# Two float16 sums moved from GpSimd to VectorE, loads one half further ahead and a store on ScalarE's queue, in a retention and PReLU kernel

## The chip, the core and the metric

One core of a Trainium2 chip runs the kernel. The metric is the device time of one execution in microseconds (us). The core's engines are named as in the profile: PE (TensorE matmuls) with PEld (its weight loads), DVE (VectorE), ACT (ScalarE), POOL (GpSimd) and SP (SyncE, which here only issues DMAs).

## What is computed

A retention recurrence over 768 tokens for 4 batches and 8 heads of width 64, then a two-layer network on all 3072 tokens:

```python
for t in range(S):
    state = gamma[None, :, None, None] * state + np.einsum('bhd,bhe->bhde', k[:, :, t], v[:, :, t])
    y[:, :, t] = scale * np.einsum('bhd,bhde->bhe', q[:, :, t], state)
x = np.ascontiguousarray(y.transpose(0, 2, 1, 3)).reshape(B * S, H * D)
h = x @ w_in                                              # 512 -> 2048
g = np.maximum(h, 0.0) + alpha * np.minimum(h, 0.0)
out = g @ w_out                                           # 2048 -> 512
```

## The kernel before

**Units, halves, blocks.** The 3072 tokens are 12 units of 256 (three to a batch). A unit has two halves, so there are 24 halves, numbered `w` from 0 to 23 in the code; from `w` = 8 on a half is 128 tokens of all heads. Two units make a block of 512 tokens; there are six blocks, `n` = 0 to 5. The recurrence is computed in chunks: products within a chunk, and a state carried from chunk to chunk.

**The way of a half.** `load` (L145) issues three DMAs on SP's queue, for k, q and v. `prep` (L190) scales k and q into float16 on POOL (four instructions at L201), issues a DMA transpose on SP's queue (L224) that waits for them, and casts v on POOL (L231). `both` (L570) then runs on PE the products of one unit that is finished ("old": L614, L590) and of one that begins ("new": scores L638, state sums L652). Its DVE part follows: the mask (L695) and six small instructions that make the next states (L707 to L713). The next call of `both` reads those states on PE at L590.

**The two layers.** `ffn1` (L739) makes, for each of 16 slices of 128 of the 2048 features, a product of four matmuls into one of eight PSUM banks (L780). ACT writes relu of its negative (L736, three buffers), and DVE joins both into `gt`, float16 (the PReLU, L725). In the prediction "PReLU 0" to "PReLU 15" are these DVE instructions of a block, in order. Blocks 0 and 1 take the second layer as plain matmuls (`ffn2`). Blocks 2 to 5 take it as seven products of half-size parts (`sevens`, L866), a Strassen scheme: `gt` falls into four quarters a11 (features 0 to 7, first 256 tokens), a21 (same features, other tokens), a12 and a22 (features 8 to 15), and these sums are needed:

- s3 = a11 - a21 (called `three[n]`, L1148), read by product 7;
- s2 = a22 - s3 (L918) and s1 = a21 + a22 (L919), for products 6 and 5;
- s4 = a12 - s2 (L927), for product 3.

Each sum is two instructions of 128x1024 float16 elements (`combine`, L845, recorded at L848). Before the change s2 and s1 run on DVE; s3 of blocks 2 to 5 and s4 of blocks 2, 3 and 4 run on POOL; s4 of block 5 runs on DVE.

**The order.** It is written out by hand: each engine executes its instructions in the order in which the program issues them, and generators (`tick`) interleave the two layers with the rest. In a block from 2 on, the first layer's 64 matmuls are issued in two lots of 20 with an `ahead` call after each; then the 40 that have been issued are ten slices, s3 follows, then the last 24. After it the products come in the order 1, 7, `both`, 2, 4, 5, the first four matmuls of 6, `both`, the rest of 6, and 3 (block 4 has the second `both` without a new unit; block 5 has the products 1, 7, 2, 6, 5, 4, 3 and no `both`). Product 1 writes the PSUM bank that slice 10 of the first layer used, and product 7 that of slice 14, so product 7 waits for PReLU 14.

`ahead(m)` (L1111) preps the next m halves and then issues the load of the half two further on for each. Block 2 preps halves 14 and 15 in its first layer, 16 and 17 beside the products; block 3 preps 18, 19 and then 20, 21; block 4 preps 22 and 23. SP takes its queue strictly in order, so a load that is issued behind a transpose waits until POOL has made what that transpose reads.

**The end.** In block 5 the results leave in stores of 256 x 256 (`store`, L911), the last of them, c12, cut in three, of which the second is issued by ACT and the others by SP.

Of the kernel before, what the change touches and what calls it, by code (L numbers as in the profile page):

```python
# [15 lines left out]
SUB = mybir.AluOpType.subtract  # L16
# [3 lines left out]
def kernel(  # L20
# [16 lines left out]
    nc = tc.nc  # L37
# [6 lines left out]
    NW = 2 * B * NUS  # L44
# [95 lines left out]
    def place(w):  # L140
        u, g = divmod(w, 2)
        b, c3 = divmod(u, NUS)
        return u, g, b, c3

    def load(w, which="kqv"):  # L145
        u, g, b, c3 = place(w)
        t = staged.setdefault(w, {})
        for nm in which:
            src = {"k": k, "q": q, "v": v}[nm]
            t[nm] = sbp.tile([128, 4, 2 * D], FP, tag=f"{nm}s", bufs=8, name=f"{nm}s{w}")  # L150
            if w < NPE:
                nc.sync.dma_start(
                    out=t[nm],
                    in_=src[b, 4 * g : 4 * g + 4, TU * c3 : TU * c3 + TU, :].rearrange(
                        "h (p a) d -> p h (a d)", a=2
                    ),
                )
            else:
                at = TU * c3 + 128 * g
                nc.sync.dma_start(  # L160
                    out=t[nm].rearrange("p a (b d) -> p (a b) d", b=2),
                    in_=src[b, :, at : at + 128, :].rearrange("h p d -> p h d"),
                )
# [675 lines left out]
    three = {}  # L839
# [5 lines left out]
    def combine(eng, out, one, two, op, at=(0, 4)):  # L845
        for i in at:
            cut = slice(i, i + 4)
            eng.tensor_tensor(out=out[:, cut], in0=one[:, cut], in1=two[:, cut], op=op)  # L848
# [17 lines left out]
    def sevens(n, ts, last=False):  # L866

        gt = gts.pop(n)  # L870
        a11, a21, a12, a22 = [quarter(gt, i, j) for i in range(2) for j in range(2)]
        ss = {1: a11, 2: a12, 4: a22, 7: three.pop(n), 5: new_part("s1"), 6: new_part("s2")}
        banks = {}
        cuts = [(0, 0, 256), (1, 0, 128), (1, 128, 128)]

        def product(m, at, start):
            steps = [(kt, t, 0, 256) for kt in range(8) for t in range(2)]
            split = last and m in (5, 3)
            if split:
                steps = [(kt, *cut) for cut in cuts for kt in range(8)]  # L880
            for i, (kt, t, c, w) in enumerate(steps):
                to = (t, c) if split else at
                first = start and i in ((0, 8, 16) if split else (0,))
                if first:
                    banks[to] = ps("ops", {(0, 0): at, (1, 0): "pb", (1, 128): "s"}[to] if split else at)
                z = 256 * t + c
                nc.tensor.matmul(  # L887
                    out=banks[to][:, z : z + w],
                    lhsT=ss[m][:, kt, 128 * t : 128 * t + 128],
                    rhs=ts[m][:, kt, c : c + w],  # L890
                    start=first,
                    stop=(kt == 7),
                    skip_group_check=True,
                )
                if i % 2:
                    yield

        def piece(name):
            return sbp.tile([128, 512], FP, tag="os", bufs=7, name=name)

        def copied(at, name):
            x = piece(name)
            nc.scalar.activation(out=x, in_=banks[at], func=COPY, bias=0.0, scale=1.0)  # L903
            return x

        def added(eng, name, one, two, cut=slice(0, 512), x=None):
            x = piece(name) if x is None else x
            eng.tensor_tensor(out=x[:, cut], in0=one[:, cut], in1=two[:, cut], op=ADD)  # L908
            return x

        def store(x, i, j, t=slice(0, 2), c=slice(0, 256), on=None):  # L911
            row = TB * n + 256 * i
            (on or nc.sync).dma_start(
                out=out[row : row + 256, 256 * j : 256 * j + 256].rearrange("(t p) c -> p t c", p=128)[:, t, c],
                in_=x.rearrange("p (t c) -> p t c", t=2)[:, t, c],
            )

        combine(nc.vector, ss[6], a22, ss[7], SUB)  # L918
        combine(nc.vector, ss[5], a21, a22, ADD)  # L919
        by = "f" + "ba"[flip["f"]]  # L920
        at = "fb" if by == "fa" else "fa"
        yield from product(1, at, True)
        x1 = copied(at, "x1")
        yield from product(7, by, True)
        x7 = copied(by, "x7")
        ss[3] = new_part("s4")
        combine(nc.vector if last else nc.gpsimd, ss[3], a12, ss[6], SUB)  # L927
        yield from product(2, at, False)
        store(copied(at, "c11"), 0, 0)
        if last:  # L930
            yield from product(6, "pa", True)
            u2 = added(nc.vector, "u2", banks["pa"], x1)
            yield from product(5, at, True)
            y = piece("y5")
            for t, c, w in cuts:
                z = 256 * t + c
                added(nc.vector, "", banks[t, c], x7, slice(z, z + w), y)
            store(added(nc.gpsimd, "c22", y, u2), 1, 1)
            yield from product(4, by, False)
            store(added(nc.vector, "c21", banks[by], u2), 1, 0)  # L940
            c12 = piece("c12")
            for i, _ in enumerate(product(3, at, False)):
                if i % 4 == 3:
                    t, c, w = cuts[i // 4]
                    z = 256 * t + c
                    added(nc.vector, "", banks[t, c], u2, slice(z, z + w), c12)
                    store(c12, 0, 1, slice(t, t + 1), slice(c, c + w), nc.scalar if i == 7 else None)
                yield
            return
        yield from product(4, by, False)  # L950
        x74 = copied(by, "x74")
        yield from product(5, at, True)
        y = added(nc.vector, "y5", banks[at], x7)
        yield from product(6, by, True)
        u2 = added(nc.vector, "u2", banks[by], x1)
        store(added(nc.gpsimd, "c21", x74, u2, x=x74), 1, 0)
        store(added(nc.gpsimd, "c22", y, u2, x=y), 1, 1)
        yield from product(3, at, False)
        store(added(nc.vector, "c12", banks[at], u2), 0, 1)
        flip["f"] = by != "fa"  # L960

    def tick(gen, m):
        for _ in range(m):
            if next(gen, 1) == 1:
                return
# [89 lines left out]
    gen = ffn1(0, "ffyppsYffSppyfsY", 2)  # L1055
# [36 lines left out]
    gen = ffn2(0, ((0, 1, 2), (3,)), ("fa", "fb", "pa", "fa"), held=held)  # L1092
# [18 lines left out]
    def ahead(m=1):  # L1111
        ws = [w for w in range(more[0], more[0] + m) if w < NW]
        for w in ws:
            prep(w)
        for w in ws:
            if w + 2 < NW:
                load(w + 2)
            while w >= 12 and held:
                to, src = held.pop(0)
                nc.sync.dma_start(out=to, in_=src)  # L1120
        more[0] += m
# [6 lines left out]
    gen = ffn1(1, "1y023Y1023sy1S0Y", 6)  # L1128
# [6 lines left out]
    for n in range(1, NBLK):  # L1135
        if n > 1:
            gen = ffn1(n, "fspyfSpY" if n == 2 else "syfSpYfp")
        for i in range(2):
            tick(gen, 10 if n == 1 else 20)
            ahead()  # L1140
            if n == 1 and i == 0:
                next(todo)
        if n == 2:
            ts = next(todo)
        if n > 1:
            three[n] = new_part("s3")
            low, late = [quarter(gts[n], 0, j) for j in range(2)]
            combine(nc.gpsimd, three[n], low, late, SUB)  # L1148
        for _ in gen:
            pass  # L1150
        if n == 1:
            gen = ffn2(n)
        else:
            gen = sevens(n, ts, n + 1 == NBLK)
        u0 = 2 * (n + 1)
        if n + 1 < NBLK:
            early = n == 1
            tick(gen, 2)
            if early:
                both(None, u0)  # L1160
            if early:
                next(todo)
            ahead(2)
            tick(gen, 24 if early else 14)
            both(u0, u0 + 1)
            if early:
                next(todo)
            tick(gen, 26)
            both(u0 + 1, u0 + 2 if 2 * u0 + 4 < NW else None)
        for _ in gen:  # L1170
            pass
# [30 lines left out]
```

## Time and profile before

| | |
|---|---|
| time, median of 3 runs | 200.85 us (200.27, 200.85, 200.94) |
| time of the profiled execution | 200.22 us |
| its span, first to last instruction | 198.5 us |
| PE busy | 191.3 us, 96% of the span |
| DVE busy | 150.1 us, 76% |
| POOL busy | 132.1 us, 67% |
| ACT busy | 97.2 us, 49% |
| granted PE clock | full in every one of 40 slices |
| POOL, one s3 instruction (L848) | 2129 ns (median of 8) |
| POOL, one s4 instruction (L848) | 2119 to 2567 ns, median 2175 (6 of them) |
| DVE, the same kind of sum (L848) | 679 to 3052 ns, median 684 |

How to read it: busy time is the time in which an engine had an instruction in flight. For PE that includes the tail of a pipelined matmul, so where PE lost time is read from stretches of equal work, not from its share. The difference between the execution's own time and its span, 1.7 us, lies before the first and after the last instruction of the program. The stages of the two layers, as used in the prediction, begin with the first L780 matmul of a block (first layer) and the first L887 matmul (products).

### The profile page before, as it was taken

What the parts mean: (1) busy time and instruction counts of PE and PEld (TensorE: products, weight loads), DVE (VectorE), ACT (ScalarE), POOL (GpSimd) and SP (SyncE); (2) the same over time, 40 slices, a digit from 0 to 9 for tenths busy, and PEclk for the clock granted to TensorE, in tenths of its full rate; (3) what the DMA queues carried; (4) which work ended last, traced back from release to release, by engine and by line L of the source; (5) the groups of instructions that cost most, each with busy time, mean ns of one, the idle gap of its engine ahead of it and who ended that gap; (6) DMA issues with size and microseconds to landing.
All of it is one profiled execution on the core that took longest, in us unless ns stands there. A gap on an engine that the chain in (4) does not pass through costs nothing. (4 is left out here: it accounts for less than half of the span.)

```text
span 198.5 us, 6106 instructions
## 1 busy us (share of the span) xinstructions
PE 191.3 (96%) x2535; PEld 122.1 (62%) x2535; DVE 150.1 (76%) x242; ACT 97.2 (49%) x166; POOL 132.1 (67%) x161
## 2 busy tenths in 40 slices
PE   6889999999999999999999999998999999999992
PEld 2667445556885455444788544887544888445892
DVE  3575887655789956788996788999988854788842
ACT  2585776245676232576353367252366352566300
POOL 3489796858799982399996699981499271371020
PEclk9999999999999999999999999999999999999999
DMA  5999999999999969999639969999263010400014
GB/s 157 319 341 338 392 376 387 395 319 222 212 226 203 230 117 217 301 315 221 153 72 222 243 189 172 224 116 237 77 196 73 0 56 3 160 0 3 0 56 159
DMA packets 90476, 38.21 MB, mean 192 GB/s; under 512 B 68288, under 2 KB 85840, under 8 KB 90448
## 3 DMA queue, kind: packets, MB, share of 16 engines
q1 hardware_dynamic: 90128, 37.69, 74.1%
q8 instruction: 20, 0.33, 0.7%
q10 hardware_dynamic: 320, 0.12, 0.3%
q14 instruction: 8, 0.07, 0.1%
HBM read 27.32 MB, written 6.29 MB: 169 GB/s over the span
## 5 line engine op out<-in xcount | busy, mean ns | idle before, releaser
L725 DVE SCALAR_TENSOR_TENSOR gt<-hm,oma,hps 128x512 f16<-128x512 f32 (+1 forms) x112 | 73.1, 670 | 13.6 <-ACT hm L736 4.8
L736 ACT ACTIVATE hm<-hps 128x512 f32<-128x512 f32 x96 | 57.2, 597 | 32.7 <-PE hps L780 28.6
L780 PE MATMUL hps<-xT,win 128*128 128x512 f16 x320 | 70.3, 379 | 0.1
L780 PEld LDWEIGHTS <-win 128*128 128x128 f16 x320 | 31.2, 98 | 37.3 <-issue 0.6
L805 PE MATMUL ops<-wout,gt 128*128 128x512 f16 x128 | 29.3, 379 | 0.0
L887 PEld LDWEIGHTS <-s 128*128 128x128 f16 x272 | 25.2, 98 | 2.8
L201 POOL TENSOR_TENSOR kdq<-ks,tab 128x256 f16<-128x256 f32 x32 | 19.9, 642 | 9.2 <-DMA ks<-in_k_dram 8.9
L887 PEld LDWEIGHTS <-gt 128*128 128x128 f16 x192 | 18.5, 98 | 3.2
L805 PEld LDWEIGHTS <-gt 128*128 128x128 f16 x128 | 11.9, 98 | 13.2
L848 POOL TENSOR_TENSOR s<-gt 128x1024 f16<-128x1024 f16 x8 | 16.9, 2129 | 4.7 <-DVE gt L725 4.7
L201 POOL TENSOR_TENSOR kdq<-qs,tab 128x256 f16<-128x256 f32 x32 | 19.4, 629 | 0.6 <-DMA qs<-in_q_dram 0.6
L848 POOL TENSOR_TENSOR s<-gt,s 128x1024 f16<-128x1024 f16 x6 | 13.5, 2266 | 4.6 <-PE ops L887 3.9
L887 PE MATMUL ops<-wout,s 128*128 128x256 f16 (+1 forms) x136 | 15.3, 266 | 0.0
L887 PE MATMUL ops<-wout,gt 128*128 128x256 f16 x128 | 15.3, 273 | 0.0
L887 PE MATMUL ops<-t,s 128*128 128x256 f16 (+1 forms) x136 | 15.3, 266 | 0.0
L763 PE MATMUL hps<-xT,win 128*128 128x256 f16 x128 | 15.2, 273 | 0.0
L908 POOL TENSOR_TENSOR x<-x,u 128x512 f32<-128x512 f32 x3 | 3.8, 1271 | 15.8 <-DVE u L908 12.5
L695 DVE TENSOR_TENSOR m<-sc,mi 128x1024 f16<-128x1024 f32 x8 | 9.8, 1219 | 4.7 <-PE sc L638 4.7
L763 PEld LDWEIGHTS <-win 128*128 128x128 f16 x128 | 12.0, 98 | 2.0
L824 ACT ACTIVATE os<-ops 128x512 f32<-128x512 f32 x8 | 4.7, 596 | 16.1 <-PE ops L805 14.8
L188 POOL CAST wout<-wo 128x512 f16<-128x512 f32 x16 | 10.3, 660 | 2.9 <-DMA wo<-in_moe_w_out_dram 2.8
L903 ACT ACTIVATE x<-ops 128x512 f32<-128x512 f32 x11 | 6.6, 596 | 9.4 <-PE ops L887 9.4
(90 smaller groups left out, 229.5 us busy)
## 6 DMA issues: line engine op xcount, KB each, us to landing
ks<-in_k_dram SPq DMA_DIRECT2D x24, 256.0 KB, 4.6
qs<-in_q_dram SPq DMA_DIRECT2D x24, 256.0 KB, 4.8
vs<-in_v_dram SPq DMA_DIRECT2D x24, 256.0 KB, 4.5
wi<-in_moe_w_in_dram SPq DMA_DIRECT2D x16, 256.0 KB, 5.8
wo<-in_moe_w_out_dram SPq DMA_DIRECT2D x16, 256.0 KB, 5.5
out_dram<-c SPq DMA_DIRECT2D x9, 256.0 KB, 2.7
out_dram<-os SPq DMA_DIRECT2D x8, 256.0 KB, 3.4
out_dram<-x SPq DMA_DIRECT2D x3, 256.0 KB, 2.2
```

The costliest lines, as they stand in the source:

```text
L188: nc.gpsimd.tensor_copy(out=dst, in_=t)
L201: eng.tensor_tensor(out=kdq[:, kind, 2 * i : 2 * i + 2].rearrange("p x r d -> p r x d"), in0=src[:, 2 * i : 2 * i + 2].rearrange("p r (x d ...
L695: nc.vector.tensor_tensor(out=m2.rearrange("p (s i) -> p s i", i=64), in0=sc.rearrange("p (s i) -> p s i", i=64), in1=mask64.unsqueeze(1). ...
L725: nc.vector.scalar_tensor_tensor(out=gt[:, ft, lo : lo + hps.shape[1]], in0=hm, scalar=oma_sb[:, ft : ft + 1], in1=hps, op0=MULT, op1=ADD,)
L736: nc.scalar.activation(out=hm, in_=hps, func=RELU, bias=0.0, scale=-1.0)
L763: nc.tensor.matmul(out=bank[:, 256 * x : 256 * x + 256], lhsT=w_in_all[:, hp, 128 * ft : 128 * ft + 128], rhs=tokens[:, hp // 2, 2 * t : 2 ...
L780: nc.tensor.matmul(out=hps, lhsT=w_in_all[:, hp, 128 * ft : 128 * ft + 128], rhs=tokens[:, hp // 2, :, hp % 2, :], start=(hp == 0), stop=( ...
L805: nc.tensor.matmul(out=opss[tq], lhsT=gt[:, ft, 128 * tq : 128 * tq + 128], rhs=w_out_all[:, ft, at], start=(ft == 0), stop=(ft == NFT - 1),)
L824: nc.scalar.activation(out=os_sb, in_=opss[tq][:, cut], func=COPY, bias=0.0, scale=1.0)
L848: eng.tensor_tensor(out=out[:, cut], in0=one[:, cut], in1=two[:, cut], op=op)
L887: nc.tensor.matmul(out=banks[to][:, z : z + w], lhsT=ss[m][:, kt, 128 * t : 128 * t + 128], rhs=ts[m][:, kt, c : c + w], start=first, stop ...
L903: nc.scalar.activation(out=x, in_=banks[at], func=COPY, bias=0.0, scale=1.0)
```

## The change

It does three things. s3 of blocks 3, 4 and 5 and s4 of blocks 3 and 4 are made by DVE; block 2 keeps both on POOL. s3's two instructions, which stood together after ten slices of the first layer, now stand one after slice 9's PReLU and one after slice 10's (four matmuls, one slice, are issued after each); this holds for block 2 too, where they are on POOL and keep their place. The load of half `w` + 3 is issued where half `w` + 2 was, from `w` = 16 on, and at `w` = 15 both are issued: half 18 is loaded in block 2's first layer, halves 19 and 20 beside block 2's products, 21 and 22 in block 3's first layer, 23 beside block 3's products. And in block 5 the store of c22 is issued by ACT and no more by SP.

```diff
@@ in sevens
-        combine(nc.vector if last else nc.gpsimd, ss[3], a12, ss[6], SUB)
+        combine(nc.gpsimd if n == 2 else nc.vector, ss[3], a12, ss[6], SUB)
...
-            store(added(nc.gpsimd, "c22", y, u2), 1, 1)
+            store(added(nc.gpsimd, "c22", y, u2), 1, 1, on=nc.scalar)
@@ in ahead
-            if w + 2 < NW:
-                load(w + 2)
+            for l in range(w + (2 if w < 16 else 3), w + (3 if w < 15 else 4)):
+                if l < NW:
+                    load(l)
@@ in the loop over the blocks
-            combine(nc.gpsimd, three[n], low, late, SUB)
+            for i in (0, 4):
+                combine(nc.gpsimd if n == 2 else nc.vector, three[n], low, late, SUB, (i,))
+                tick(gen, 4)
```

## The prediction, as put on record before the changed kernel ran

> **What bounds the kernel now.** First the page's engine shares:
>
> ```profile
> PE 191.3 (96%) x2535; PEld 122.1 (62%) x2535; DVE 150.1 (76%) x242; ACT 97.2 (49%) x166; POOL 132.1 (67%) x161
> ```
>
> PE is hardly ever without work, so an edit on DVE or POOL pays only where PE loses time. To find that place I read busy time by stage: first layer and products of blocks 2 to 5, in turn.
>
> ```profile
> 81.60:95.41 13.81, 13.81 (x65) 6.23 (x64) 11.46 (x18) 9.55 (x16) 10.88 (x9) 1.00 1.05 256
> 95.41:110.35 14.94, 14.94 (x354) 13.11 (x353) 13.06 (x20) 5.33 (x9) 12.00 (x13) 1.00 0.67 151
> 110.35:124.16 13.81, 13.81 (x66) 6.23 (x64) 11.37 (x17) 8.96 (x15) 13.49 (x17) 1.00 0.93 196
> 124.16:140.31 16.15, 15.49 (x362) 13.37 (x361) 15.58 (x20) 5.33 (x9) 9.99 (x11) 1.00 1.15 198
> 140.31:154.42 14.11, 13.97 (x66) 6.24 (x64) 12.29 (x19) 8.96 (x15) 12.36 (x14) 1.00 0.34 96
> ```
>
> The columns after the stretch are its length, then busy us (and count) of PE, PEld, DVE, ACT and POOL. Block 3's products take 16.15 us where block 2's take 14.94, for nearly the same matmuls, and the first layer after them 14.11 against 13.81. So PE loses 1.21 + 0.30 = 1.5 us there and next to nothing in the other stages. PE's waits inside 134 to 144 us name who is late:
>
> ```profile
> PE sums L652 <- DVE tg L713: 0.4, 1, 0.4
> PE y L590 <- DVE tg L707: 0.2, 1, 0.2
> ```
>
> PE waits for the states, which DVE makes; DVE is busy 15.58 of these 16.15 us. The timeline (start, duration, instruction) says what with:
>
> ```profile
> 125.66 4.07 DVE L848 TENSOR_TENSOR s<-gt,s 128x1024 f16<-128x1024 f16 x2
> ...
> 129.65 3.21 DVE L848 TENSOR_TENSOR s<-gt 128x1024 f16<-128x1024 f16 x2
> 129.87 4.97 POOL L848 TENSOR_TENSOR s<-gt,s 128x1024 f16<-128x1024 f16 x2 [0.69 <-DVE s L848]
> ...
> 155.92 1.28 DVE L848 TENSOR_TENSOR s<-gt,s 128x1024 f16<-128x1024 f16 x2
> 157.12 1.29 DVE L848 TENSOR_TENSOR s<-gt 128x1024 f16<-128x1024 f16 x2
> ```
>
> The four instructions of s2 and s1 need 2.5 us in block 4, where POOL is idle, and 7.2 us (125.66 to 132.86) in block 3, where POOL runs the preps of halves 20 and 21 and then s4. In block 2, also beside preps, they take 4.2. So a float16 sum on DVE and POOL's instructions hold each other up, while a PReLU stays at 746 to 749 ns whatever POOL does. The mask and the states start only at 132.78: that is the delay that PE pays for.
>
> **The change, part by part.** All sums are made against the profiled execution, 200.22 us (span 198.5 and 1.7 around it); the median of the runs shown, 200.85, is 0.63 above.
>
> *s3 and s4 leave POOL.* POOL loses ten instructions of 2.1 to 2.6 us. In block 3 this frees 118.81 to 122.98 (s3), so prep 20 can start at 118.81 and not at 122.98, and prep 21 behind it. One prep there takes 2.85 us (122.98 to 125.83), two end at 124.5 instead of 129.18. PReLU 15 ends at 125.74, so s2 and s1 find POOL idle: 2.5 us, as in block 4, and not 7.2. The mask then starts near 129 (its scores are ready at 128.6) and not at 132.78, the states are there by 133, s4 on DVE (1.28) by 134.3, ahead of the sum of product 5 that follows it. The waits at 135 to 137 go. What is late next in that stage is nothing that I can find: PE's own 14.94. The 0.30 in block 4's first layer go too, since c12's sum on DVE, which freed a bank at 142.49, comes earlier. **Gain 1.5 us**; block 3's stage has a few more small state products than block 2's (32 against 24), so I count **1.4**.
>
> *s3 on DVE in the first layer.* A slice needs 13.81 / 16 = 0.863 us of PE. A PReLU that follows another at once takes 0.66 (three in 2.06 us at 142.41), so DVE has 0.20 to spare per slice; a sum without POOL takes 0.60 (two in 1.28). After s3's first instruction DVE is 0.60 - 0.20 = 0.40 late, after the second 0.80, and 0.20 less with each later slice: 0.2 late at PReLU 14 and none at 15. Product 7 waits for PReLU 14: in block 3 this ends at 124.88 and the product starts at 125.91, a cover of 1.0 us (the same in blocks 4 and 5: products at 156.17 and 184.27, PReLU 14 ends at 155.14 and 183.24). So without POOL s3 costs **nothing**; if the cover were gone, PE would pay each us of lateness. In blocks 4 and 5 POOL is idle by then (preps 22 and 23 end at 150.05 and now earlier; s3 comes at 150.8, both shifted alike). In block 3 it is not: PReLU 9 ends at 120.56 (125.74 less six slices of 0.863), amid preps 20 and 21. The rows for such a meeting are the eight sums of blocks 2 and 3 on DVE: one of 0.68 (no wait), five of about 1.09 (it waits out the POOL instruction under way, then has its turn; all four of block 2), one of 2.61 (a turn behind an s4 instruction of 2.4), and one of 3.05, when DVE stood behind four more POOL instructions. Taking turns means 0.4 more for each, 1.0 late at PReLU 14: a stall of **0 to 0.15**. I take 0.1. Held as in the 3.05 row: below.
>
> The Trainium skill (GPSIMD Engine Reference, section 1 Specifications) says that POOL shares its SBUF interfaces with VectorE and that they contend when a DVE instruction has two SBUF inputs; by this rule s3 meets preps 20 and 21 in block 3, which speaks against the change, and the PReLUs, with one input in PSUM, do not. Its page Advanced Engine Details and Errata (VectorE Performance Modes) names only two-port modes, by which these sums would cost 0.68 everywhere and the stall would be nought. The 7.2 us against 2.5 bear out the first.
>
> *s4 on DVE.* In block 3 priced above; in block 4 it stands between the states (last one ends 161.87) and a wait of 2.83 us before 164.69, which covers 1.28. **Nothing.**
>
> *Loads.* No DMA is added. Half 18's three (issue 0.58, 0.58, 0.9 us) go from SP's queue at 104.0 to 94.63, where SP is idle until the transpose at 98.52. They land by about 100.5 (half 17's landed 0.9 apart up to 97.76), so transpose 16 may land 1 to 2 us later than 101.24; PE reads it at 106.47, with that of 17, which landed at 105.43 and is issued at 102.72 as before. So nothing there. Half 20 lands by 112.72, in the place of 19; half 21's v at 121.88, in the place of 20. Prep 20 and 21 (from 121.67) thus find their data, without which the gain of the first part would be gone: with loads two ahead, half 20's v landed at 121.88 and 21's at 127.97. What it costs: load 22 stands ahead of transposes 20 and 21 on SP, so they are issued near 124.7 and 126, against 125.34 and 128.19. **Nothing**, bounded above by 0.5 (transpose 20 took 6.9 us behind a load; half 21 is read at 134.7 now).
>
> *The store.* At the end SP issues c22 at 193.19, c21 at 193.94 (0.85 long), c12's pieces from 194.88 and 195.39; DVE's last sum ends at 195.28. Without c22 SP may be free 0.1 sooner for the last piece. On ACT's queue only the middle piece stands behind c22, 1.3 us later. The last landing comes 2.0 us after its issue either way. **0 to 0.1 gained**, I take 0.05.
>
> Sum: -1.4 + 0.1 - 0.05 = **-1.35**: 198.9 from the profiled execution, 199.5 from the median. How much of the 0.63 between them stays I can't tell (the slower runs may hold longer meetings of DVE and POOL, which would go); I take the middle, **199.1**.
>
> **The rivals.** *1. Held once.* In block 3 s3's first sum asks when PReLU 9 ends, 120.56, some 0.02 us before a POOL instruction ends (prep 20's begin 0.57 apart from 118.81 and overlap by 0.05); the sum that took 3.05 asked at 125.74, 0.13 before a POOL instruction ended, the first of block 2 at 96.99, 0.48 before. That speaks for it; that six of the seven meetings were turns speaks against. Four more POOL instructions pass, it starts at 122.86 and ends at 123.4, PReLU 10 at 124.1, the second sum, one turn, at 125.2, PReLU 14 at 127.9: product 7 stalls 1.95. Net -1.35 + 1.85 = +0.5: 200.7, no change to be measured (that limit is 0.3%, 0.6 us).
>
> *2. Held to the end, slower.* Same place; POOL does not let go before its preps end at 124.55. Then the first sum ends at 125.15, PReLU 10 at 125.8, the second sum at 126.4 and PReLU 14 at 129.0, a stall of 3.1 us: +1.65, 201.9. If the first is held once and the second to the end, PReLU 14 ends at 128.4, stall 2.5, 201.3. It decides for slower from a stall of about 2.1 us, that is PReLU 14 later than 128.0.
>
> *3. The work does not leave as planned.* The built program shows the ten sums on DVE where the text puts them, so it does what it says; but the transposes 20 and 21 could land late behind load 22 (they took 5.0 and 6.9 us before), and PE would then wait at 134.7 for them instead of for the states. From 1 us late the gain is mostly gone: 199.9 to 200.5.
>
> **How the numbers follow.** Forecast (turns or no meeting): 0.60, time 199.1, own range 198.5 to 199.7. Rival 1: 0.16. Rival 2: 0.16. Rival 3: 0.08. Leaving out the worst of rival 2 (about a tenth) and a tenth below, the range is 198.5 to 201.3. Faster by over 0.3%: 0.60. Within: 0.20 (rival 1, half of 3). Slower: 0.20 (rival 2, the rest).
>
> **What would show it.** Right: block 3's products at about 15.0 us and block 4's first layer at 13.8; s2 and s1 of block 3 at 0.68 each; PE's waits for L707 and L713 after 134 gone. Wrong: a PE wait of product 7 on PReLU 14 near 126 us with an L848 instruction of 2 us or more before it; a wait of L638 or L652 for a transpose; blocks 4 or 5 whose product 7 waits, which would say that 0.20 us to spare per slice was misread.

## The result and the profile after

The changed kernel takes 202.61 us (median of 12 runs, 200.26 to 203.73), the kernel before, beside it, 200.41: a ratio of 1.0094 (95% interval 1.0066 to 1.0123). It is slower where I forecast faster, and its time lies above my range. Ratios here leave out the executions over 1.5% above the fastest of the same kernel, so of a kernel whose times fall into two groups the ratio sees the lower group alone.

The profiled execution took 202.41 us, with a span of 200.2; that of the kernel before 200.22 and 198.5. The engine shares of the changed kernel:

```profile
PE 190.8 (95%) x2535; PEld 121.9 (61%) x2535; DVE 153.8 (77%) x252; ACT 97.2 (49%) x166; POOL 109.4 (55%) x151
```

POOL lost 22.7 us and DVE gained 3.7; PE does the same work in a longer span. Busy time by stage of the changed kernel (columns as before: length, then PE, PEld, DVE, ACT and POOL; products of block 2, first layer and products of block 3, first layer and products of block 4):

```profile
95.27:110.69 15.42, 15.07 (x354) 13.18 (x353) 12.63 (x20) 5.33 (x9) 13.27 (x13) 1.00 0.92 199
110.69:126.14 15.45, 13.97 (x66) 6.27 (x64) 13.59 (x15) 7.76 (x13) 13.87 (x22) 1.00 0.96 231
126.14:142.48 16.34, 15.01 (x361) 13.12 (x361) 14.87 (x26) 6.41 (x11) 0.00 (x0) 1.00 0.48 109
142.48:156.37 13.89, 13.89 (x67) 6.26 (x65) 12.76 (x20) 8.96 (x15) 8.19 (x12) 1.00 0.34 96
156.37:170.72 14.35, 14.35 (x298) 12.63 (x296) 10.15 (x18) 5.42 (x11) 0.66 (x1) 1.00 0.06 21
```

Against before, in this order: +0.48, +1.64, +0.19, -0.22, +0.10; block 5 gives back 0.3 and all that is ahead 0.15. So the span grew by 1.74, and 0.44 more lie outside it (2.16 against 1.72). The waits of PE from 112 to 145 us (total, number, longest) name one cause:

```profile
PE ops L887 <- DVE gt L725: 2.8, 2, 1.5
```

and from 94 to 112 us one small one, "issue", in which PE waits for nothing that the profile shows:

```profile
PE ops L887 <- issue: 0.3, 1, 0.3
```

The waits for L707 and L713, which the change was to remove, are gone. Two waits for a PReLU have come. The timeline of DVE around them (start, duration, instruction):

```profile
118.42 2.48 DVE L725 SCALAR_TENSOR_TENSOR gt<-hm,oma,hps 128x512 f16<-128x512 f32 x3
120.81 4.62 DVE L848 TENSOR_TENSOR s<-gt 128x1024 f16<-128x1024 f16 x1
125.35 0.73 DVE L725 SCALAR_TENSOR_TENSOR gt<-hm,oma,hps 128x512 f16<-128x512 f32 x1
126.01 0.68 DVE L848 TENSOR_TENSOR s<-gt 128x1024 f16<-128x1024 f16 x1
126.61 3.37 DVE L725 SCALAR_TENSOR_TENSOR gt<-hm,oma,hps 128x512 f16<-128x512 f32 x5
129.90 1.28 DVE L848 TENSOR_TENSOR s<-gt,s 128x1024 f16<-128x1024 f16 x2
131.11 1.28 DVE L848 TENSOR_TENSOR s<-gt 128x1024 f16<-128x1024 f16 x2
```

and of PE:

```profile
126.14 1.91 PE L887 MATMUL ops<-wout,gt 128*128 128x256 f16 x16 [1.48 <-DVE gt L725]
129.38 0.82 PE L887 MATMUL ops<-t,s 128*128 128x256 f16 x6 [1.33 <-DVE gt L725]
```

s3's first sum, 0.68 us of work, takes 4.62. PReLU 9, ahead of it, ends at 120.90, so the sum asks then. POOL's preps 20 and 21 run without a gap until this instruction ends, at 124.88, and the sum ends 0.55 later:

```profile
124.27 0.61 POOL L231 CAST vx<-vs 128x512 f16<-128x512 f32 x1
```

PReLU 10 to 14 queue behind the sum on DVE. Product 1 waits 1.48 us for PReLU 10, whose bank it writes, and product 7 another 1.33 for PReLU 14. This is rival 2. I call such a sum **held**, and say that a sum **has its turn** when it waits only for the POOL instruction under way (beside the preps 0.7 to 1.2 us in all). s2 and s1, at 129.90, take 1.28 a pair, POOL being idle, as forecast.

### The profile page after: what moved, and what is told of

Read it like the earlier page. It is cut to its first block, busy times and chain, and to the rows that moved or that the text cites. A ratio compares the mean times of both kernels' runs of the same rounds, so it can differ in the third digit from the quotient of the medians.

```text
span 200.2 us, 6096 instructions
## 1 busy us (share of the span) xinstructions
PE 190.8 (95%) x2535; PEld 121.9 (61%) x2535; DVE 153.8 (77%) x252; ACT 97.2 (49%) x166; POOL 109.4 (55%) x151
## 4 chain that ended last, share of the span: by engine, by line
PE 86%; DVE 5%; SPq 4%; DMA 3%; issue 1%; POOL 0%; ACT 0%
PE hps L780 32%; PE ops L887 24%; PE ops L805 14%; PE hps L763 7%; SPq L152 4%; DMA vs<-in_v_dram 3%; DVE s L848 3%; DVE gt L725 2%; PE y L614 1%; PE sc L638 1%; PE sums L652 1%; PE y L590 1%; PE trb L259 1%; PE y L392 1%; PE y L372 0%
## 5 line engine op out<-in xcount | busy, mean ns | idle before, releaser
L725 DVE SCALAR_TENSOR_TENSOR gt<-hm,oma,hps 128x512 f16<-128x512 f32 (+1 forms) x112 | 72.2, 669 | 11.4 <-ACT hm L736 5.4
L201 POOL TENSOR_TENSOR kdq<-qs,tab 128x256 f16<-128x256 f32 x32 | 19.9, 643 | 0.0
L887 PE MATMUL ops<-wout,gt 128*128 128x256 f16 x128 | 15.5, 273 | 1.8 <-DVE gt L725 1.5
L848 DVE TENSOR_TENSOR s<-gt 128x1024 f16<-128x1024 f16 x14 | 14.0, 1024 | 0.0
L908 POOL TENSOR_TENSOR c<-y,u 128x512 f32<-128x512 f32 x1 | 1.3, 1269 | 21.4 <-DVE y L908 21.4
L188 POOL CAST wout<-wo 128x512 f16<-128x512 f32 x16 | 10.1, 649 | 3.5 <-DMA wo<-in_moe_w_out_dram 3.4
L188 POOL CAST win<-wi 128x512 f16<-128x512 f32 x16 | 9.8, 616 | 1.4 <-DMA wi<-in_moe_w_in_dram 1.0
```

Source lines behind the costliest of these rows:

```text
L188: nc.gpsimd.tensor_copy(out=dst, in_=t)
L201: eng.tensor_tensor(out=kdq[:, kind, 2 * i : 2 * i + 2].rearrange("p x r d -> p r x d"), in0=src[:, 2 * i : 2 * i + 2].rearrange("p r (x d ...
L725: nc.vector.scalar_tensor_tensor(out=gt[:, ft, lo : lo + hps.shape[1]], in0=hm, scalar=oma_sb[:, ft : ft + 1], in1=hps, op0=MULT, op1=ADD,)
L887: nc.tensor.matmul(out=banks[to][:, z : z + w], lhsT=ss[m][:, kt, 128 * t : 128 * t + 128], rhs=ts[m][:, kt, c : c + w], start=first, stop ...
```

## The experiments

Unless said otherwise each kernel is the changed one with the edit shown; "before" is the kernel before in the same comparison, and a ratio is the time against it. Of each kernel one execution has a trace: stages, waits and sums are of that one, and what the sums did in the other executions is known only from their times (of the changed kernel's 12, one took 200.26 us).

**1. Which part costs it.** *The sums back on POOL, loads and store as changed:*

```diff
-        combine(nc.gpsimd if n == 2 else nc.vector, ss[3], a12, ss[6], SUB)
+        combine(nc.vector if last else nc.gpsimd, ss[3], a12, ss[6], SUB)
-                combine(nc.gpsimd if n == 2 else nc.vector, three[n], low, late, SUB, (i,))
+                combine(nc.gpsimd, three[n], low, late, SUB, (i,))
```

> Loads and the store as in the changed kernel, all sums on the engines of the kernel before. Theory 1: within 0.6 us of the kernel before, 200.2 to 201.0, of which up to 0.5 is a gap of PE at 102 us that waits for nothing but its instructions, if the loads cause it. Rival 1: 202 or more, without any sum moved.

201.6 us, ratio 1.0007 (0.997 to 1.0044); the time lies above the 200.2 to 201.0 of my theory and below the 202 of the rival. Block 3 is nearly as it was: first layer 13.81, products 16.31, PE waits for the states, and s2's first sum is held for 3.63 us, until POOL has run dry. But block 2's products take 15.75 instead of 14.94; PE waits there 0.4 us for "issue" and 0.2 for a transpose.

*The loads back to two ahead, the rest as changed:*

```diff
-            for l in range(w + (2 if w < 16 else 3), w + (3 if w < 15 else 4)):
-                if l < NW:
-                    load(l)
+            if w + 2 < NW:
+                load(w + 2)
```

> The changed kernel without its loads: they are two halves ahead, as before. Theory 1a: POOL then waits for the data of halves 20 and 21 between 121 and 126 us, and DVE gets in at the first gap, so s3's first sum takes 2 us at most and product 7 waits under 0.8; but s2 and s1 meet prep 21; 199.3 to 200.8. Rival 1 (the sums on DVE cost by themselves, whatever POOL does): 202 or more.

199.29 us, ratio 0.9946 (0.9913 to 0.998): **without the loads' move the change is faster than before.** Its timeline of POOL shows why; the preps of halves 20 and 21 wait for their data:

```profile
119.03 0.62 POOL L231 CAST vx<-vs 128x512 f16<-128x512 f32 x1
121.00 1.63 POOL L201 TENSOR_TENSOR kdq<-ks,tab 128x256 f16<-128x256 f32 x2 [1.35 <-DMA ks<-in_k_dram]
```

s3's sums there take 0.88 and 1.01 us, s2 and s1 0.68 to 1.10; block 3 takes 13.81 and 14.85.

*c22's store back on SP's queue:* `on=nc.scalar` left out.

> The changed kernel with the store of c22 back on SP's queue. Time outside the span is 2.15 us in the changed kernel and 1.72 in the kernel before; if the store on ACT makes that difference, it is about 1.7 here and the time 202.2; if not, 2.15 and 202.6. The waits near 126 stay in both.

202.31 us, ratio 1.0084 (1.005 to 1.0119), s3 held for 4.59 us: the store is not it. Block 2's products take 14.94 here although the loads are moved, so the loss in block 2 does not come with them in every execution. The time outside the span stays, at 2.28.

**2. Is the held sum the loss?** *Preps 20 and 21 wait for s3* (the meeting is taken away, the sum stays where it is):

```diff
+                ins = combine(nc.gpsimd if n == 2 else nc.vector, three[n], low, late, SUB, (i,))
+                if n == 3:
+                    gate[20] = ins
... in prep, at its first POOL instruction
+                    if (kind, i) == (0, 0) and w in gate:
+                        behind(ins, gate[w], "s3 goes first")
```

> The changed kernel, with prep 20's first instruction on POOL made to wait for s3's second sum of block 3, so that POOL is idle while s3 runs. Theory 1: both sums of s3 take 0.68, no wait of product 1 or 7; preps 20 and 21 run from about 122 to 128 and meet s2 and s1, which end by about 130.5, before the mask's states are needed at 134.7; 199.2 to 200.3. Rival 1: 202 or more, since the loads stay where they are.

199.46 us, ratio 0.9888 (0.9838 to 0.9938). s3's sums on DVE:

```profile
121.95 0.69 DVE L852 TENSOR_TENSOR s<-gt 128x1024 f16<-128x1024 f16 x1
...
123.21 0.68 DVE L852 TENSOR_TENSOR s<-gt 128x1024 f16<-128x1024 f16 x1
```

No wait of PE from 112 to 145 us; block 3 takes 13.81 and 14.85. The delayed preps cost nothing that these stages show. *The same with the store on SP:*

> The changed kernel, with preps 20 and 21 behind s3 (as in the run where prep 20 waits for s3) and the store of c22 on SP. Theory 1: 199.2 to 199.8, some 1.2 under the kernel before, no wait of products 1 and 7; if the store matters, 0.1 to 0.4 under the run with it on ACT.

199.23 us, ratio 0.9933 (0.99 to 0.9966).

*s3 of block 3 on POOL again* (`n <= 3` for `n == 2` in its `combine`):

> The changed kernel, with s3 of block 3 alone back on POOL; s4 of blocks 3 and 4 and s3 of blocks 4 and 5 stay on DVE. Theory 1 (s3's first sum in block 3 is held on DVE until POOL has run out of preps, and product 1 and product 7 wait for the PReLUs behind it): both waits near 126 and 129 us go (2.8 us), preps 20 and 21 start near 123 again and meet s2 and s1, but no s4 on POOL follows; 199.5 to 200.7. Rival 1 (the loss comes from the loads that were moved, through the DMA queues or the instruction fetch): 202 to 202.6, as the changed kernel. Rival 2 (DVE has no room in the first layer): also faster, but then blocks 4 and 5 must show waits, too.

200.53 us, ratio 0.997 (0.9935 to 1.0005). In the profiled execution, the longest of the ten (203.36), s3 no longer holds DVE up, but the next meeting does: s2's first sum takes 3.61 us, until POOL stands still, and block 4's first layer 14.76. **The hold moves to the next sum that meets the preps.**

**3. What decides between a turn and a hold?** My first theory was rival 1's: the moment of asking, so close to the end of a POOL instruction that the turn is missed. Two memsets of one element ahead of s3 make it ask later:

```diff
+                for _ in range(2 if (n, i) == (3, 0) else 0):
+                    nc.vector.memset(warm[0:1], 0.0)
```

> The changed kernel, with two memsets of one element (59 ns each in the profile of before) added on DVE right before s3's first instruction of block 3. They compute nothing. That sum then is issued some 0.1 us later, just behind the start of the next POOL instruction and not 0.05 us ahead of it. Theory 1a (the moment of asking decides, with a turn for whoever asks at least 0.25 us before POOL's next instruction starts): it gets its turn after that instruction, 1.1 to 1.2 us, and the added work makes the kernel 2.5 us faster, 199.3 to 200.2. Theory 1b (not the moment but the unbroken run of preps in front of it): held to the end again, 202.3 to 203.

202.68 us, ratio 1.0086 (1.0046 to 1.0127): held for 4.46 us, though it asked 0.47 us ahead of POOL's next instruction. The moment alone is not it. In this kernel block 2's products take 16.06, and PE waits there 0.8 us for transposes.

*s3 one slice earlier:*

```diff
-            tick(gen, 10 if n == 1 else 20)
+            tick(gen, 10 if n == 1 else 16 if (n, i) == (3, 1) else 20)
```

> The changed kernel, with s3 of block 3 one slice earlier (behind PReLU 8 and PReLU 9), so that the first sum asks 0.3 us before a POOL instruction ends and not 0.02. Theory 1a (the moment of asking decides): it gets its turn, 1.1 us, the waits near 126 shrink to under 0.5, 199.6 to 200.4. Theory 1b (once DVE has lost a turn, or whenever POOL has its next instruction ready, it is held until POOL runs dry): the first sum ends near 125.4 again, now with one PReLU more behind it, 202.5 to 203.3. Rival 1: unchanged, 202.6.

199.44 us, ratio 0.9934 (0.99 to 0.9968); s3's sums take turns, with prep 20 still beside them:

```profile
120.96 0.93 DVE L848 TENSOR_TENSOR s<-gt 128x1024 f16<-128x1024 f16 x1
121.81 0.73 DVE L725 SCALAR_TENSOR_TENSOR gt<-hm,oma,hps 128x512 f16<-128x512 f32 x1
122.47 1.01 DVE L848 TENSOR_TENSOR s<-gt 128x1024 f16<-128x1024 f16 x1
```

*Two slices earlier* (12 for 16):

> The changed kernel, with s3 of block 3 two slices earlier (behind PReLU 7 and PReLU 8). Two slices (1.73 us) are nearly three POOL instructions (1.71), so the first sum asks again within 0.05 us of the end of a POOL instruction, as in the changed kernel. Theory 1a (the moment decides): it is held again until POOL runs dry near 125, with two PReLUs more behind it than in the changed kernel; products 1 and 7 wait 4 to 5 us in all, 203.5 to 205. Rival (an earlier s3 is simply better, since DVE has more slices in which to catch up): 199 to 199.8, like the one that was one slice earlier, or better.

199.82 us, ratio 0.9984 (0.9956 to 1.0012), where the moment of asking had called for 203.5 or more. The sum asked at the end of one POOL instruction and the start of the next (119.04 us), waited that next one out and had its turn (1.22 us, then 1.01); PE waited 0.7 us in the first layer for a PReLU.

*One slice earlier and three memsets:*

> The kernel with s3 of block 3 one slice earlier (which got its turns), with three such memsets right before s3's first instruction of block 3. It is then issued about 0.15 us ahead of POOL's next instruction, where it was 0.33 ahead. Theory 1a: held for several POOL instructions, up to the end of the preps near 126.8; 202 to 204.5. If it is let in after one more instruction, as in the run two slices earlier, 199.6 to 200.5. Theory 1b has no reason for a difference: 199.4.

Ten runs in two groups: five from 199.3 to 200.8 (ratio 0.9946, 0.9911 to 0.9981), five from 204.9 to 206.7. The profiled one is of the second; s3 was held for 5.19 us. So this kernel seems to stand at a threshold; that s3 has its turn in the first group is not shown, no trace being of it.

*The kernel before, with three memsets ahead of s2 of block 3:*

> The kernel before, with three such memsets on DVE right before s2's first instruction of block 3, which took 3.05 us and was issued 0.17 us ahead of POOL's next instruction. It is then issued at or just behind the start of that instruction. Theory 1a: it takes about 1.2 us, s2 and s1 are through 1 to 2 us sooner, PE's waits at 135 to 137 shrink from 1.2 to under 0.5: 199.3 to 200.2. Theory 1b: unchanged or 0.1 slower, 200.4.

200.58 us, ratio 0.9958 (0.9915 to 1.0001): no difference that is clear of the spread (198.57 to 203.94). In the profiled execution (198.77 us) s2 and s1 take turns, and block 3's products 14.85 instead of 16.15:

```profile
126.12 1.05 DVE L848 TENSOR_TENSOR s<-gt,s 128x1024 f16<-128x1024 f16 x1
...
127.10 1.10 DVE L848 TENSOR_TENSOR s<-gt,s 128x1024 f16<-128x1024 f16 x1
128.12 2.12 DVE L848 TENSOR_TENSOR s<-gt 128x1024 f16<-128x1024 f16 x2
```

So in this execution the stall that the change was to remove is gone with the held sum (3.05 us) and the meeting with s4 behind it (2.61).

*A sweep by itself:* 50 meetings of two DVE sums with 18 POOL instructions; memsets of 8 to 620 columns set the moment. It leaves out the whole computation, as do the sweeps below.

> Not the computation: it leaves out the whole of it, and times 50 meetings of DVE and POOL by themselves (the output is not the reference's). In each, POOL runs fourteen of the preps' scaling instructions and four casts back to back; DVE is released by the first of them, spends a memset of 8 to 620 columns (a step of 25 columns, two series) and then issues two float16 sums of 128x1024. Theory 1a (the moment of asking within a POOL instruction decides): the first sum is 0.7 to 1.3 us at most moments and several us, up to POOL's last instruction, in one connected range of moments, about the last 0.2 us before POOL's next instruction. Theory 1c (the moment matters, but as a race that is decided by more than the moment): long and short ones lie mixed at the same moment. Theory 1b (an unbroken run of POOL instructions holds DVE always): all are long.

The first sums (L88) and second sums (L89), start and duration in the timeline of the sweep:

```profile
15.58 10.12 DVE L88 TENSOR_TENSOR s<-one,two 128x1024 f16<-128x1024 f16 x1
25.62 0.68 DVE L89 TENSOR_TENSOR s<-one,two 128x1024 f16<-128x1024 f16 x1
...
27.16 1.01 DVE L88 TENSOR_TENSOR s<-one,two 128x1024 f16<-128x1024 f16 x1
28.10 1.09 DVE L89 TENSOR_TENSOR s<-one,two 128x1024 f16<-128x1024 f16 x1
...
38.31 10.07 DVE L88 TENSOR_TENSOR s<-one,two 128x1024 f16<-128x1024 f16 x1
```

So it goes 50 times, in strict alternation, whatever the moment: a turn (0.63 to 1.07 us), then held until POOL has run dry (9.5 to 10.1). What came earlier decides. I took it for the last meeting: a lone DVE sum in between would set it back. *The sweep with such a sum* (it waits for POOL's last instruction, and POOL's next trial for it):

> The sweep of 50 meetings again (it leaves out the whole computation of the reference), with one more VectorE sum in every trial: it waits for GpSimd's last instruction of the trial, and GpSimd's next trial waits for it, so that VectorE always sums alone between two meetings. Theory 'the last meeting decides': all 50 first sums take a turn (0.6 to 1.1 us), none 9.5 to 10.1 us; the span is near 50 x 11.5 us = 575 us or below. Rival 'it alternates by itself': 25 of them are held for 9.5 to 10.1 us as in the sweep. Rival 'chance': a mixture without the strict alternation.

All 50 are turns. The groups of DVE (busy us, mean ns):

```profile
L89 DVE TENSOR_TENSOR s<-one,two 128x1024 f16<-128x1024 f16 x50 | 54.6, 1091 | 0.0
L88 DVE TENSOR_TENSOR s<-one,two 128x1024 f16<-128x1024 f16 x50 | 39.1, 781 | 1.0 <-DVE s L90 0.8 <-DVE fill L65 0.2
```

But in the changed kernel a lone sum of 128x128 while POOL stands still changed nothing:

> The changed kernel with one more VectorE instruction: a float16 sum of 128x128 with two inputs in SBUF, beside block 2's products just ahead of the sum u2, where GpSimd stands still (108.5 to 111.0 us in the changed kernel's trace). It costs VectorE about 0.15 us where it waits for TensorE anyway. Theory 'the last meeting decides' (a sum is held if, at the meeting before, GpSimd's take-over came while VectorE was still asking; it has its turn if VectorE last summed alone): the first sum of s3 in block 3 now takes 0.7 to 1.3 us instead of 4.6, product 1 doesn't wait for a PReLU (1.48 us in the changed kernel), block 3's first layer is 13.8 us and not 15.46; time 199.3 to 200.5. Rival 'something else, by chance or by the exact cycle': held 4.4 to 4.7 us as in the four kernels that differ from the changed one only at the edges; time 202.0 to 202.9.

```profile
110.13 0.22 DVE L957 TENSOR_TENSOR spare<-ones 128x128 f16<-128x128 f16 x1
...
120.76 4.73 DVE L849 TENSOR_TENSOR s<-gt 128x1024 f16<-128x1024 f16 x1
```

Seven of ten runs took 202.0 us or more (median 202.24); the ratio, 1.0009 (0.9959 to 1.0058), is of the six shortest. A lone sum from which POOL took over directly (`behind` from c21's sum to it) changed nothing either:

> The changed kernel with one more VectorE sum of two inputs in SBUF (128x384 float16, about 0.3 us) beside block 2's products, right behind u2, and GpSimd's next instruction, the sum c21, waits for it: the order of events of the second sweep. Theory 'the last meeting decides, set back by a lone sum from which GpSimd takes over': s3's first sum in block 3 takes 0.6 to 1.1 us, no wait of product 1 for a PReLU, 199.5 to 200.8. Rival 'a run too long' (the sum asks some 16 GpSimd instructions after the pause here, at the second one in the sweep) or a cause that the sweeps don't hold: held 4.4 to 4.8 us, 202.0 to 203.2.

202.71 us, ratio 1.0098 (1.006 to 1.0135), held for 4.87 us. The second sweep had changed two things: the lone sum, and a pause of POOL shortly ahead of each meeting. *Two sweeps tell these apart:* 30 POOL instructions after a pause, and one DVE sum that asks after the 1st, 2nd, ... 24th of them; the pause is a memset in one, a lone DVE sum in the other.

```diff
+            late = nc.vector.memset(fill[:, 0:width], 0.0)
+            behind(late, made[at - 1], "the trial begins")
+            nc.vector.tensor_tensor(out=s3[0], in0=one, in1=two, op=SUB)
+            last = nc.vector.memset(fill[:, 0:600], 0.0)
+            behind(last, made[-1], "POOL stands still")
```

> 48 meetings of one float16 sum of 128x1024 on VectorE with 30 GpSimd instructions back to back (it leaves out the whole computation of the reference). The sum asks after GpSimd's instruction 1, 2, ... 24 since its pause, in 24 trials with a memset of 8 columns ahead of it and 24 with one of 300; between the trials GpSimd stands still for a memset, and VectorE does no lone sum. Theory 'the pause is enough': all 48 take 0.6 to 1.1 us. Theory 'a run too long': turns up to some count of instructions, held (until GpSimd's 30th, so shorter the later it asks) above. Theory 'the last meeting decides, and only a lone sum sets it back': held and turn alternate, or held whenever the trial before was a turn, whatever the count.

The sums that ask after the 11th to 16th instruction, from the timeline of DVE:

```profile
193.51 1.07 DVE L89 TENSOR_TENSOR s<-one,two 128x1024 f16<-128x1024 f16 x1 [6.42 <-issue]
212.42 1.07 DVE L89 TENSOR_TENSOR s<-one,two 128x1024 f16<-128x1024 f16 x1 [6.99 <-issue]
231.33 1.62 DVE L89 TENSOR_TENSOR s<-one,two 128x1024 f16<-128x1024 f16 x1 [7.56 <-issue]
250.23 1.05 DVE L89 TENSOR_TENSOR s<-one,two 128x1024 f16<-128x1024 f16 x1 [8.13 <-issue]
269.12 9.01 DVE L89 TENSOR_TENSOR s<-one,two 128x1024 f16<-128x1024 f16 x1 [8.68 <-issue]
288.00 8.43 DVE L89 TENSOR_TENSOR s<-one,two 128x1024 f16<-128x1024 f16 x1 [9.25 <-issue]
```

The idle time in brackets is about the time since POOL's pause. Asking after the 1st to 12th, the sum has its turn. After the 13th one more POOL instruction passes, after the 14th the sum has its turn again, and **from the 15th on it is held until POOL has run dry** (9.01, 8.43, ... 3.88 us: each starts 0.57 us later and ends at the same point). The 24 trials with the longer memset, which ask 0.3 us later, break at the same place.

> The same 48 meetings (it leaves out the whole computation too), but the pause between two trials is a VectorE sum of two inputs in SBUF that runs alone, as in the second sweep. Theory 'the last meeting decides': all 48 take a turn, 0.6 to 1.1 us, whatever the count. Theory 'a run too long': turns up to some count, held above, the same count as without the lone sum. Theory 'the pause is enough': all turns here and without the lone sum.

With the lone sum: the same place, every duration within 20 ns. The lone sum does nothing; the length of POOL's run since its last pause, or since it last gave way, does. This also fits the alternation in the first sweep: after a trial of turns POOL ran on into the next trial without a pause, after a held trial it had waited for DVE.

*The test in the kernel:* POOL pauses once (1.18 us), 3.3 us ahead of the meeting, which stays.

```diff
+                    ins = prelu(gt, ft, 0, hps, minus(hps))
+                    if (n, ft) == (3, 5):
+                        gate[19] = ins
... in prep, at its first POOL instruction
+                    if (kind, i) == (0, 0) and w in gate:
+                        behind(ins, gate[w], "GpSimd pauses")
```

> The changed kernel, but GpSimd's first instruction of prep 19 (116.31 us in the changed kernel's trace) waits for PReLU 5 of block 3 (ends 117.45): a pause of 1.1 us, after which GpSimd has run only 3.5 us and six or seven instructions when s3's first sum asks at 120.9. The meeting itself stays: the preps of halves 19 to 21 run beside s3 and end 1.1 us later than before. Theory 'a run too long' (from 8.6 us in the sweeps, between 9.03 and 9.20 us in the kernels): s3's sums take 0.7 to 1.1 us, product 1 and 7 wait for no PReLU, block 3's first layer 13.8 and its products 14.85 to 15.1 us; time 199.0 to 200.3. Rival 'held for another cause': held until GpSimd is dry, now 5.5 us or more, the wait of product 1 and 7 some 3 to 4 us; time 202.3 to 203.7.

POOL's timeline shows the pause and the preps that meet s3 (in pairs of 1.63 us instead of 1.18):

```profile
117.28 1.18 POOL L202 TENSOR_TENSOR kdq<-ks,tab 128x256 f16<-128x256 f32 x2 [1.18 <-DVE gt L728]
...
120.12 1.63 POOL L202 TENSOR_TENSOR kdq<-ks,tab 128x256 f16<-128x256 f32 x2
121.72 1.63 POOL L202 TENSOR_TENSOR kdq<-qs,tab 128x256 f16<-128x256 f32 x2
```

and DVE's that s3 has its turns:

```profile
120.58 0.71 DVE L853 TENSOR_TENSOR s<-gt 128x1024 f16<-128x1024 f16 x1
121.21 0.73 DVE L728 SCALAR_TENSOR_TENSOR gt<-hm,oma,hps 128x512 f16<-128x512 f32 x1
121.87 1.01 DVE L853 TENSOR_TENSOR s<-gt 128x1024 f16<-128x1024 f16 x1
```

199.33 us (198.69 to 202.17), 198.99 in the profiled execution, block 3 at 13.81 and 14.93, no wait of PE from 94 to 145 us. The median lies 3.3 us under the changed kernel's (the kernel before took 200.56 beside this one, 200.41 beside that); against before the ratio is 0.9978 (0.9932 to 1.0024), so that it beats the kernel before is not shown, whose runs spread from 198.44 to 203.49 here.

Count POOL's instructions from its last pause to the one under way when the sum asks (a sum that asks after the 12th asks in the 13th). The first sums of the meetings are then:

| where | instruction | outcome |
|---|---|---|
| sweeps | 2nd to 13th | turn |
| sweeps | 14th / 15th | one passes, then a turn / turn |
| sweeps | 16th to 25th | held to the end |
| block 2, every kernel | 9th to 12th | turn |
| block 3, paused kernel | 6th | turn |
| block 3, loads two ahead | 1st | turn |
| block 3, s2, preps behind s3 (both kernels) | 6th | turn |
| block 3, two slices earlier | 12th or 13th, at the border | turn behind the 13th |
| block 3, one slice earlier, without / with memsets | 14th | turn / held |
| block 3, changed kernel and four like it | 15th, 16th | held to the end |
| block 3, s2, sums back on POOL and s3 of block 3 on POOL | 19th | held to the end, 3.6 us |
| block 3, s2, kernel before | 19th | four pass, then a turn |
| block 3, s2, kernel before with memsets | 20th | turn |

The count orders these better than the time does: in block 2 POOL's run was 11 to 13 us old at a turn, in the changed kernel 9.9 at a hold. But no run separates the number of POOL's instructions from their kind. At the border the sweeps and the kernels differ: a sum in the 15th has its turn in the sweeps and is held in two kernels. And the last two rows don't fit. So the limit is not the whole rule, and why POOL stops giving way stays open.

## Why the prediction was wrong, point by point

- **What bounds the kernel: right**, as far as it went. PE lost 1.5 us to late states in block 3, and s2 and s1 beside the preps made them late. That a held sum of 3.05 us, and not the mass of work on DVE, had made them late (with three memsets, in the one execution profiled, it has its turn and the stage falls to 14.85) I had not seen, though the row was there.
- **s3 and s4 leave POOL: right in size.** s2 and s1 take 0.64 each, the waits for the states are gone, block 4's first layer falls from 14.11 to 13.89. Without the two new waits (15.45 - 13.81 in the first layer, 1.33 in the products) blocks 3 and 4 would stand at -1.26 against before; I had -1.4.
- **s3 in the first layer: the step that failed** is "Taking turns means 0.4 more for each, 1.0 late at PReLU 14: a stall of 0 to 0.15. I take 0.1." I chose the turn by counting rows, six of seven, and they were not rows of the same thing: four came right after a meeting in which POOL had just given way, one in the first instruction of a run of POOL, one in the 12th. The one late in a run, in the 19th, was the 3.05, and the new meeting comes in the 15th or 16th. The term, the stall behind s3, is 2.97 us instead of 0.1: s3 is held until POOL has run dry. For a turn it was right: where s3 takes turns, product 7 doesn't wait.
- **The rivals.** Rival 2 named the mechanism, the place and nearly the numbers: preps' end 124.55 (124.88), end of the sum 125.15 (125.43), time 201.9 (202.41). Its sum, +1.65, is met by what the stalls and the gains of blocks 3 and 4 give, 2.97 - 1.26 = +1.71; the rest of the 202.41 (0.48 in block 2, 0.44 outside the span, 0.45 gained elsewhere) was in no sum. It missed that product 1 waits first, for PReLU 10, so that the stall comes in two; its chance, 0.16, was too low. Rival 1's reason, the moment of asking, fell with the two memsets and the sweep. Rival 3 didn't happen: no wait for transposes 20 and 21.
- **Which DVE instructions meet POOL: right.** Beside the preps s3's sum takes 4.62 us instead of 0.68, while PReLUs take 735 to 750 ns with POOL at work and without. The Trainium skill (GPSIMD Engine Reference, section 1 Specifications) has a DVE instruction with two SBUF inputs contend with POOL; the trace agrees. The Trainium skill (SBUF — State Buffer, SBUF: two separate sides) says more: whichever of the two starts first has the shared port pair for its whole instruction, and the other blocks. The turns agree with that (0.7 to 1.2 us); a hold over six whole POOL instructions goes beyond it, and there the measurement decides.
- **The loads: wrong once, the other open.** I counted only for the change that preps 20 and 21 find their data. That is what removed POOL's pauses: with the old loads POOL waits 1.35 us ahead of prep 20, and s3 has its turns. And for block 2 I said nothing, bounded by 0.5. Its products took 0.48 more in the profiled execution, 0.8 and 1.1 more in two other kernels with the loads moved, and at most 0.2 more in all others. That the loads did it is not shown. In these three executions, and in no other, POOL was late: it ended the scaling for transpose 16 at 4.7 to 5.9 us into the stage (2.7 to 3.9 elsewhere), since it began prep 15 only 9.4 to 10.1 us ahead of the stage (10.5 to 11.3 elsewhere), and that was 10 us or more before the first moved load was issued. Transposes 16 and 17 were so issued late, and where PE waits for them they also took 3.6 to 6.5 us to land (2.7 before), which the loads may have caused. The two gaps named "issue" (0.3 and 0.4 us) stay unexplained.
- **s4, blocks 4 and 5: right.** PE has no wait there; s2 and s1 of block 4 take 1.29 a pair. The store's 0 to 0.1 is not shown: what follows the start of block 5's products is 0.27 shorter than before (15.72 against 15.99), but it is 15.56 with the store back on SP's queue, and from 15.5 to 16.1 over all the kernels.
- **Outside the span: not foreseen, and open.** 0.44 us. Seven kernels, the kernel before among them, show 1.7 to 1.8 there and nine 2.1 to 2.3 in their profiled executions; neither the store (2.28 without it), nor the sums (1.74 with them), nor the loads (1.73 with them) separates them.

## What to carry to other kernels

Where DVE takes float16 sums with two inputs in SBUF beside POOL, ask how many instructions POOL will have run without a pause when the sum asks. In these runs it cost one POOL instruction early in such a run, and after some fourteen nearly always all that POOL had left. Making POOL's data early is then no free good, since its waits for data were the pauses in which DVE came in. When a few rows are to say what a new meeting costs, compare how each came about instead of counting them: the one bad row among seven was the one that resembled the new case.

## What the runs showed of the hardware that was not expected

A long wait of PE cost more than its length. In the kernel with three memsets and s3 one slice earlier PE waited 4.0 us for a PReLU; busy time of three stretches there, before, in and after the wait; each row ends with granted clock, DMA share and GB/s:

```profile
111.26:122.50 11.24, 11.24 (x54) 5.09 (x52) 9.38 (x15) 7.16 (x12) 10.92 (x17) 1.00 0.95 235
122.50:127.00 4.50, 0.46 (x2) 0.10 (x1) 4.50 (x3) 0.27 (x1) 2.93 (x6) 0.75 1.11 227
127.00:131.66 4.66, 4.66 (x13) 1.62 (x11) 3.69 (x6) 1.52 (x3) 0.00 (x0) 0.51 1.17 164
```

After the wait the granted clock is 0.51, and 128x512 matmuls start 427 ns apart instead of 216, for over 4 us. The first layer takes 20.40 us instead of 13.81, so beside the 4.04 of the wait another 2.55 are lost. The Trainium skill (TensorE: Matmul & The Clock Gate, Part 1) has the gate fall to half rate after an idle window; this trace agrees, while after the waits of 1.48 and 1.33 us in the changed kernel the granted clock stayed at 1.00. So a stall of 4 us is worth more than its length in a prediction's sum; this is one wait of one execution. The waits for PReLUs in the other kernels, of 1.7 us at most, left the clock at 1.00.
